# Experts' weighted sums: from a VectorE multiply-add to a ScalarE scaling and an accumulating DMA from GpSimd's queue

## The chip, the cores and the metric

The kernel runs on one core of a Trainium2 chip. The metric is the device time of one execution in microseconds (us). Three executions of the kernel before took 652.2, 653.46 and 654.13 us, so the median is 653.46 us.

## The reference, cut to what matters

Three stages follow one another. A windowed attention (2 batches, 8 heads, 576 positions) gives `x` of 1152 tokens by 512. A mixture of four experts, all of them used for every token, turns `x` into a weighted sum. A last stage with a rational activation turns that into the output.

```
p = domain_probs / (domain_probs.sum(-1, keepdims=True) + 1e-09)
out = np.zeros((N, D), dtype=np.float32)          # N = 1152, D = 512
for e in range(E):                                # E = 4, F = 1024
    h = np.maximum(x @ w1[e], 0.0)
    out += p[:, e:e + 1] * (h @ w2[e])            # the weighted sums of the change
x = out
h = x @ w_in                                      # 512 -> 2048
g = (a0 + a1 h + a2 h^2 + a3 h^3) / (1 + |b0||h| + |b1| h^2 + 1e-06)
return g @ w_out                                  # 2048 -> 512
```

## The kernel before, in words

The 1152 tokens are nine tiles of 128 (t = 0 to 8) in three chunks of three (c = 0 to 2). Each matrix operand is split into a high and a low part, and three products are summed for each, so that float32r matmuls give nearly float32 precision. The hidden units are walked in groups g of 512: groups 0 to 7 belong to the four experts (two groups each), groups 8 to 11 to the last stage. A group has two halves u = 2g and 2g + 1.

For each group and chunk the kernel does three things. `h_bank` (line 321) makes the first products of a half in PSUM tiles called `ps_h`, 24 matmuls for a half and chunk. `h_relu` has ScalarE write the rounded positive part `hh` (line 334), and VectorE the rest `hl` (line 335). `o_tile` (through `o_half`, line 358) makes the second product of one token tile, 12 matmuls into one PSUM bank `ps_o`; the pool `pso` has two such banks. Then `o_sum` adds that bank into the token tile's accumulator `acc[t]`, an SBUF tile of 128 by 512 float32. For the experts, group 0 is written by a VectorE multiply (line 380), and groups 1 to 7 are added by one VectorE instruction that multiplies the bank by the token's expert weight and adds it to `acc[t]` (line 382). That is 7 groups by 9 tiles, 63 instructions.

Between the experts and the last stage stands the turn: `x2_turn` (line 403) has TensorE transpose the three finished accumulators of a chunk into PSUM, and `x2_split` cuts the result into the high and low operands of the next products. The order there, written out by hand at `g == NG1` and just before it, is: the transposes of chunk 0 (tiles 0 to 2); `o_tile` of tiles 3, 4, 5 and then 6 of group 7; the transposes of chunk 1 (tiles 3 to 5); the first products of two halves of chunk 0; `o_tile` of tiles 7 and 8; the first products of one half of chunk 1; and the first transposes of chunk 2 (tiles 6 to 8).

The instruction order of every engine is the order in which the code issues it (`tc.manual_schedule()`); each engine runs its own queue in order and waits on semaphores for the others. SP's queue issues the weight loads (line 88 loads the last stage's weights, 1024 KB each) and the stores. Through groups 0 to 7 a side job (`convert`, lines 119 to 172) turns the last stage's 64-bit weights into float32 on VectorE and ScalarE, two steps after each `o_tile` and `h_step`. GpSimd works in the attention alone (line 260); its queue is empty afterwards.

Of the kernel before, what the change touches and what calls it, by code (L numbers as in the profile page):

```python
# [18 lines left out]
F32 = mybir.dt.float32  # L19
# [3 lines left out]
AF = mybir.ActivationFunctionType  # L23
ALU = mybir.AluOpType
# [5 lines left out]
NT, DM = 1152, 512  # L30
# [14 lines left out]
def body(ctx, tc, qkv, mask, dp, w1, w2, w1d, w2d, coef, out):  # L45
    nc = tc.nc
# [3 lines left out]
    hp = ctx.enter_context(tc.tile_pool(name="hp", bufs=6))  # L50
    wp = ctx.enter_context(tc.tile_pool(name="wp", bufs=4))
    dram = ctx.enter_context(tc.tile_pool(name="dram", bufs=1, space=DRAM))
    rawp = ctx.enter_context(tc.tile_pool(name="rawp", bufs=4))
    pso = ctx.enter_context(tc.tile_pool(name="pso", bufs=2, space=PSUM))
    psh = ctx.enter_context(tc.tile_pool(name="psh", bufs=2, space=PSUM))
# [2 lines left out]
    def h_tile(count=[0]):  # L58

        count[0] += 1  # L60
        pool = third[0] if third and count[0] % 3 == 0 else psh
        return pool.tile([128, 2, 512], F32, tag="h", name="ps_h")
# [250 lines left out]
    acc = {}  # L313
# [26 lines left out]
    def rows(t):  # L340
        if t < 3:
            return [(0, 128, S // 3 + 128 * t)]
        if t == 3:
            return [(0, 128, 0)]
        if t == 4:
            return [(0, 64, 128), (64, 64, S)]
        return [(0, 128, 128 * t)]
# [14 lines left out]
    def o_bank():  # L362
        return pso.tile([128, 512], F32, tag="o", name="ps_o")

    def o_tile(g, t, ps=None):

        held, ps = ps is not None, ps if ps is not None else o_bank()
        for v in range(2):
            o_half(g, t, v, ps)
        if not held:  # L370
            o_sum(g, t, ps)

    def o_sum(g, t, ps):
        first = g in (0, NG1)
        if first:
            acc[t] = accp.tile([128, DM], F32, tag=f"acc{t}", name=f"acc{t}")
        if g < NG1:
            pe = p_sb[:, t, g // 2:g // 2 + 1]
            if first:
                nc.vector.tensor_scalar(out=acc[t], in0=ps, scalar1=pe, scalar2=None, op0=ALU.mult)  # L380
            else:
                nc.vector.scalar_tensor_tensor(  # L382
                    out=acc[t], in0=ps, scalar=pe, in1=acc[t], op0=ALU.mult, op1=ALU.add
                )
        elif first:
            nc.vector.tensor_copy(acc[t], ps)
        else:
            nc.vector.tensor_tensor(out=acc[t], in0=ps, in1=acc[t], op=ALU.add)  # L388
        if g == NG - 1:
            for a, n, r in rows(t):  # L390
                nc.sync.dma_start(out[r:r + n, :], acc[t][a:a + n, :])
# [79 lines left out]
    with tc.manual_schedule():  # L471
# [326 lines left out]
        ps = h_tile()  # L798
        ps = [ps[:, 0], ps[:, 1], o_bank()]
# [8 lines left out]
        for t in range(3):  # L808
            o_sum(g, 3 + t, ps[t])
        ps = [h_tile()[:, 0], h_tile()[:, 0], o_bank()]  # L810
        for v in range(2):
            for t in range(3):
                o_half(g, 6 + t, v, ps[t])
                if v == 1:
                    o_sum(g, 6 + t, ps[t])
# [109 lines left out]
```

## Time and profile before

| | |
|---|---|
| median of three executions | 653.46 us (652.2 to 654.13) |
| span of the profiled execution, first to last instruction | 650.9 us |
| TensorE (PE) busy | 639.6 us, 98% |
| VectorE (DVE) busy | 485.0 us, 75% |
| ScalarE (ACT) busy | 277.7 us, 43% |
| GpSimd (POOL) busy | 17.0 us, 3% |
| granted TensorE clock | 1.000 |

For the profiled execution the profile gives the span alone and no time of its own besides; the span lies 2.6 us below the median of the three timed executions, and that difference holds what lies around the span. In the profile, PE is TensorE's matmuls and PEld its weight loads, which overlap them. A row of the timeline begins with the start and the duration in us; a bracket at its end gives the idle time before it and what ended that.

### The profile page before, as it was taken

How to read it: one execution, taken by the hardware profiler on the slowest of the kernel's cores; microseconds unless marked ns; L12 is line 12 of the kernel's file. 1: busy time of each engine (PE TensorE's matmuls, PEld its weight loads, DVE VectorE, ACT ScalarE, POOL GpSimd, SP SyncE). 2: the span in 40 equal slices, each digit the busy share in tenths (PEclk: the TensorE clock that was granted, in tenths of full speed). 3: DMA queues.
4: the chain of work that ended last, by engine and by line, in shares of the span. 5: the costliest groups of instructions: out<-in, count | busy, mean ns of one | idle time of the engine just before them, and what ended most of it. 6: DMA issues, size and time to landing. Idle time of an engine off the chain costs nothing.

```text
span 650.9 us, 9488 instructions
## 1 busy us (share of the span) xinstructions
PE 639.6 (98%) x3838; PEld 574.6 (88%) x3839; DVE 485.0 (75%) x693; ACT 277.7 (43%) x518; POOL 17.0 (3%) x30
## 2 busy tenths in 40 slices
PE   8989999999999999999999999999999999999996
PEld 4878898999999999999999999989999999999985
DVE  6767326867867777777767766436999999999986
ACT  5887412413313323223233232115666555556651
POOL 2311100000000000000000000000000000000000
PEclk9999999999999999999999999999999999999999
DMA  9973011545344444454553572431230330300012
GB/s 293 275 219 104 21 65 47 195 148 172 120 161 149 142 163 137 154 162 115 176 162 102 161 254 93 167 130 38 92 130 1 129 130 2 129 1 1 0 49 97
DMA packets 25707, 79.53 MB, mean 122 GB/s; under 512 B 2720, under 2 KB 3232, under 8 KB 23616
## 3 DMA queue, kind: packets, MB, share of 16 engines
q1 hardware_dynamic: 25376, 78.77, 37.4%
q8 instruction: 30, 0.49, 0.3%
q10 hardware_dynamic: 288, 0.16, 0.1%
q14 instruction: 13, 0.11, 0.0%
HBM read 59.79 MB, written 19.14 MB: 121 GB/s over the span
## 4 chain that ended last, share of the span: by engine, by line
PE 94%; DVE 3%; ACT 2%; issue 0%; DVEq 0%; ACTq 0%
PE ps_h L321 46%; PE ps_o L358 43%; PE ps_v L285 1%; ACT pr L250 1%; PE ps_s L271 1%; PE ps_s L218 1%; PE ps_h L403 1%; PE ps_h L547 1%; PE ps_h L358 0%; DVE u L447 0%; DVE acc L388 0%; DVE u L460 0%; DVE sq L455 0%; DVE sq L452 0%; DVE sq L437 0%
## 5 line engine op out<-in xcount | busy, mean ns | idle before, releaser
L321 PE MATMUL ps_h<-xh,w 128*128 128x384 f32 x1152 | 301.7, 336 | 2.0 <-DVE hl L335 2.0
L358 PE MATMUL ps_o<-w,hh 128*128 128x512 f32 x832 | 224.3, 391 | 0.0
L321 PEld LDWEIGHTS ps_h<-xh,w 128*128 128x128 f32 x1152 | 208.8, 188 | 3.9 <-DVE hl L335 2.2
L321 PE MATMUL ps_h<-xl,w 128*128 128x384 f32 x576 | 192.7, 335 | 0.0
L358 PEld LDWEIGHTS ps_o<-w,hh 128*128 128x128 f32 x832 | 155.1, 188 | 31.1 <-ACT hh L334 0.4
L358 PE MATMUL ps_o<-w,hl 128*128 128x512 f32 x416 | 128.6, 390 | 0.0
L321 PEld LDWEIGHTS ps_h<-xl,w 128*128 128x128 f32 x576 | 108.1, 188 | 1.2
L335 DVE SCALAR_TENSOR_TENSOR hl<-ps_h,hh 128x768 fp32r<-128x768 f32 x48 | 45.9, 957 | 73.2 <-ACT hh L334 73.2
L358 PEld LDWEIGHTS ps_o<-w,hl 128*128 128x128 f32 x416 | 78.0, 188 | 16.9 <-DVE hl L335 0.4
L334 ACT ACTIVATE hh<-ps_h 128x768 fp32r<-128x768 f32 x48 | 39.1, 814 | 120.6 <-PE ps_h L321 120.5
L168 ACT CAST w<-f 128x512 fp32r<-128x512 f32 x32 | 19.9, 621 | 123.6 <-DVE f L165 123.6
L382 DVE SCALAR_TENSOR_TENSOR acc<-ps_o,p_sb,acc 128x512 f32<-128x512 f32 x63 | 47.1, 748 | 11.4 <-PE ps_o L358 11.4
L106 DVE TENSOR_TENSOR w<-raw,w 128x512 fp32r<-128x512 f32 x64 | 42.0, 695 | 0.7 <-ACT w L105 0.6
L170 DVE TENSOR_TENSOR w<-f,w 128x512 fp32r<-128x512 f32 x32 | 22.2, 692 | 22.8 <-ACT w L168 22.8
L441 ACT ACTIVATE ab<-sq,cbias 128x768 f32<-128x768 f32 x24 | 22.6, 944 | 37.2 <-DVE sq L437 37.0
L105 ACT CAST w<-raw 128x512 fp32r<-128x512 f32 x60 | 34.0, 617 | 0.0
L432 ACT ACTIVATE sq<-ps_h 128x768 f32<-128x768 f32 x24 | 19.3, 803 | 32.4 <-PE ps_h L321 32.4
L250 ACT ACTIVATE pr<-pr,mx 128x80 f32<-128x80 f32 (+1 forms) x84 | 29.7, 356 | 6.5 <-DVE mx L243 6.3
L437 DVE SCALAR_TENSOR_TENSOR sq<-sq,absb,ab 128x768 f32<-128x768 f32 x24 | 24.3, 1011 | 3.8 <-ACT ab L433 3.8
L467 DVE TENSOR_TENSOR hl<-u,hh 128x768 fp32r<-128x768 f32 x24 | 22.9, 954 | 5.4 <-ACT hh L464 5.4
L447 DVE SCALAR_TENSOR_TENSOR u<-u,na,ps_h 128x768 f32<-128x768 f32 x24 | 24.3, 1014 | 0.9
L460 DVE SCALAR_TENSOR_TENSOR u<-u,na,sq 128x768 f32<-128x768 f32 x24 | 24.3, 1013 | 0.4
(64 smaller groups left out, 521.0 us busy)
## 6 DMA issues: line engine op xcount, KB each, us to landing
w<-w SPq DMA_DIRECT2D x32, 512.0 KB, 3.6
w<-w SPq DMA_DIRECT2D x16, 1024.0 KB, 5.4
raw<-in_w_dram SPq DMA_DIRECT2D x30, 512.0 KB, 5.9
x<-in_w1d_dram SPq DMA_DIRECT2D x16, 512.0 KB, 5.1
x<-in_w2d_dram SPq DMA_DIRECT2D x16, 512.0 KB, 5.2
out_dram<-acc SPq DMA_DIRECT2D x8, 256.0 KB, 2.2
v<-in_qkv_dram SPq DMA_DIRECT2D x6, 320.0 KB, 6.7
qk<-in_qkv_dram SPq DMA_DIRECT2D x4, 448.0 KB, 5.3
```

Of the source, the lines that this page charges most:

```text
L105: (nc.vector.tensor_copy if early else nc.scalar.copy)(w[:, 0, s], raw[:, s])
L106: nc.vector.tensor_tensor(out=w[:, 1, s], in0=raw[:, s], in1=w[:, 0, s].bitcast(F32), op=ALU.subtract)
L250: nc.scalar.activation(pr[:, j, i], pr[:, j, i], AF.Exp, scale=-1.0, bias=self.mx[:, j, i:i + 1], accum_out=self.total[:, j, i:i + 1],)
L321: nc.tensor.matmul(ps[:, i, :TC], lhsT=a[:, k, f], rhs=b[:, k], start=k + n == 0, stop=k + n == 5,)
L334: nc.scalar.activation(hh, ps[:, :, :TC], AF.Relu)
L335: nc.vector.scalar_tensor_tensor(out=hl, in0=ps[:, :, :TC], scalar=0.0, in1=hh.bitcast(F32), op0=ALU.max, op1=ALU.subtract,)
L358: nc.tensor.matmul(ps, lhsT=a[:, i, tk], rhs=b[:, i], start=v + n == 0, stop=v + n == 6)
L382: nc.vector.scalar_tensor_tensor(out=acc[t], in0=ps, scalar=pe, in1=acc[t], op0=ALU.mult, op1=ALU.add)
L437: nc.vector.scalar_tensor_tensor(out=self.sq, in0=self.sq, scalar=absb[:, 1:2], in1=self.ab, op0=ALU.mult, op1=ALU.add,)
L447: nc.vector.scalar_tensor_tensor(out=self.u1, in0=self.u1, scalar=na[:, 1:2], in1=ps, op0=ALU.add, op1=ALU.mult)
L460: nc.vector.scalar_tensor_tensor(out=self.u1, in0=self.u1, scalar=na[:, 0:1], in1=self.sq, op0=ALU.add, op1=ALU.mult)
L467: nc.vector.tensor_tensor(out=self.hl, in0=self.u1, in1=self.hh.bitcast(F32), op=ALU.subtract)
```

## The change

In groups 1 to 7 the one VectorE instruction goes. In its place ScalarE multiplies the bank by the token's expert weight and writes the product into an SBUF tile `add`, one of four in a new pool. GpSimd's queue then issues a DMA that adds `add` to `acc[t]` in SBUF. Group 0 and the last stage stay as they were.

```
+    tmpp = ctx.enter_context(tc.tile_pool(name="tmpp", bufs=4))
...
             if first:
                 nc.vector.tensor_scalar(out=acc[t], in0=ps, scalar1=pe, scalar2=None, op0=ALU.mult)
             else:
-                nc.vector.scalar_tensor_tensor(
-                    out=acc[t], in0=ps, scalar=pe, in1=acc[t], op0=ALU.mult, op1=ALU.add
-                )
+                add = tmpp.tile([128, DM], F32, tag="add", name="add")
+                nc.scalar.activation(add, ps, AF.Copy, scale=pe)
+                nc.gpsimd.dma_start(acc[t], add, accum_op=ALU.add)
```

One line is added ahead of `o_sum`, so that line 403 of the kernel before is line 404 after, and so on. The rows below are instructions in the order of one engine's queue, with what each waits for: DMASW is a DMA of GpSimd's queue, PE, DVE and Activation the engines. On ScalarE before, at the turn (`hh` are group 7's last relus, `xh0` and `xh1` the splits of chunks 0 and 1, `sq` and `ab` the last stage's first activations):

```order
L334 ACTIVATE hh_3984<-ps_h_3959 128x768 [waits PE_49]
L334 ACTIVATE hh_4015<-ps_h_3990 128x768 [waits PE_49]
L411 CAST xh0_4019<-ps_h_4021 128x768 [waits PE_49]
L411 CAST xh0_4019<-ps_h_4030 128x768 [waits PE_49]
L411 CAST xh1_4099<-ps_h_4101 128x768 [waits PE_49]
L411 CAST xh1_4099<-ps_h_4110 128x768 [waits PE_49]
L432 ACTIVATE sq_4144<-ps_h_4119 128x768 [waits DMAHW0_49,DMAHW3_49,DVE_49,PE_49]
```

On ScalarE after, at the same place:

```order
L335 ACTIVATE hh_4101<-ps_h_4076 128x768 [waits PE_49]
L335 ACTIVATE hh_4132<-ps_h_4107 128x768 [waits PE_49]
L412 CAST xh0_4136<-ps_h_4138 128x768 [waits PE_49]
L412 CAST xh0_4136<-ps_h_4147 128x768 [waits PE_49]
L384 ACTIVATE add_4169<-ps_o_4156,p_sb_87 128x512 [waits DMASW5_49,PE_49,Activation_49]
L384 ACTIVATE add_4185<-ps_o_4172,p_sb_87 128x512 [waits DMASW6_49,PE_49,Activation_49]
L384 ACTIVATE add_4201<-ps_o_4188,p_sb_87 128x512 [waits DMASW7_49,PE_49,Activation_49]
L384 ACTIVATE add_4221<-ps_o_4208,p_sb_87 128x512 [waits DMASW0_49,PE_49,Activation_49]
L412 CAST xh1_4224<-ps_h_4226 128x768 [waits PE_49]
L412 CAST xh1_4224<-ps_h_4235 128x768 [waits PE_49]
```

The four scalings of tiles 3 to 6 have come between the splits of chunks 0 and 1; their DMASW wait is for the DMA that read the same `add` tile four uses ago. On VectorE the four rows of line 382 that stood there are gone. On TensorE before, the transposes of chunk 1 (`acc3` to `acc5`) behind the last matmuls of tile 6:

```order
L358 MATMUL ps_o_4085<-w2_3609,hl_4016 128x512 x2
L403 MATMUL ps_h_4101<-ident_81,acc3_1153 128x128 [waits PE_49]
L403 MATMUL ps_h_4101<-ident_81,acc4_1178 128x128
L403 MATMUL ps_h_4101<-ident_81,acc5_1212 128x128 [waits DVE_49]
L403 MATMUL ps_h_4101<-ident_81,acc3_1153 128x128
L403 MATMUL ps_h_4101<-ident_81,acc4_1178 128x128
L403 MATMUL ps_h_4101<-ident_81,acc5_1212 128x128
```

On TensorE after:

```order
L359 MATMUL ps_o_4208<-w2_3708,hl_4133 128x512
L404 MATMUL ps_h_4226<-ident_84,acc3_1156 128x128 [waits DMASW1_49,PE_49]
L404 MATMUL ps_h_4226<-ident_84,acc4_1181 128x128 [waits DMASW2_49]
L404 MATMUL ps_h_4226<-ident_84,acc5_1215 128x128 [waits DMASW3_49]
L404 MATMUL ps_h_4226<-ident_84,acc3_1156 128x128
L404 MATMUL ps_h_4226<-ident_84,acc4_1181 128x128
L404 MATMUL ps_h_4226<-ident_84,acc5_1215 128x128
```

TensorE's own order is the same. The third transpose waited for VectorE's addition to tile 5 and now waits for the DMA that adds to it; the transposes of chunks 0 and 2 changed in the same way. The matmul that opens a `ps_o` bank again after such a sum waits for ScalarE where it waited for VectorE. On GpSimd's queue the 63 DMAs stand behind the attention's last instruction of line 260 (261 after), with nothing between them.

## Rows read from the trace of the kernel before

**Rows 1.** The page: busy time by engine, and the span in 40 slices.

```profile
PE 639.6 (98%) x3838; PEld 574.6 (88%) x3839; DVE 485.0 (75%) x693; ACT 277.7 (43%) x518; POOL 17.0 (3%) x30
...
PE   8989999999999999999999999999999999999996
```

**Rows 2.** The chain that ended last: start us, us, what; groups 6 and 7.

```profile
385.05 8.34 PE ps_h L321 x48
393.40 8.20 PE ps_o L358 x36
401.60 8.34 PE ps_h L321 x48
409.94 8.20 PE ps_o L358 x36
```

**Rows 3.** Stages: us, then busy us and instructions of each engine, clock, DMA.

```profile
115.00:455.00 340.00, 340.00 (x1736) 310.12 (x1735) 241.72 (x372) 101.70 (x158) 0.00 (x0) 1.00 0.45 147
```

**Rows 4.** Groups by line, 115 to 455 us: busy us, mean ns | idle before.

```profile
L382 DVE SCALAR_TENSOR_TENSOR acc<-ps_o,p_sb,acc 128x512 f32<-128x512 f32 x63 | 47.1, 748 | 11.4 <-PE ps_o L358 11.4
...
L334 ACT ACTIVATE hh<-ps_h 128x768 fp32r<-128x768 f32 x38 | 31.0, 815 | 104.8 <-PE ps_h L321 104.7
...
L168 ACT CAST w<-f 128x512 fp32r<-128x512 f32 x31 | 19.3, 621 | 119.6 <-DVE f L165 119.6
```

**Rows 5.** Line 382: min/median/max ns, first and last start us.

```profile
L382 DVE SCALAR_TENSOR_TENSOR acc<-ps_o,p_sb,acc x63: 742/750/753, 114.9 to 454.6; 128x512 f32<-128x512 f32 x63
```

**Rows 6.** Timeline of TensorE at 37.7 us.

```profile
37.74 0.44 PE L321 MATMUL ps_h<-xh,w 128*128 128x384 f32 x1 [1.96 <-DVE hl L335]
```

**Rows 7.** Timeline of VectorE at the turn.

```profile
418.19 0.75 DVE L382 SCALAR_TENSOR_TENSOR acc<-ps_o,p_sb,acc 128x512 f32<-128x512 f32 x1 [1.27 <-PE ps_o L358]
...
436.04 0.75 DVE L382 SCALAR_TENSOR_TENSOR acc<-ps_o,p_sb,acc 128x512 f32<-128x512 f32 x1 [1.97 <-PE ps_o L358]
```

**Rows 8.** Timeline of TensorE at the turn: transposes, and tile 8's last matmuls.

```profile
426.33 1.47 PE L403 MATMUL ps_h<-ident,acc 128*128 128x128 f32 x12
...
435.61 0.39 PE L358 MATMUL ps_o<-w,hl 128*128 128x512 f32 x1
...
438.56 1.48 PE L403 MATMUL ps_h<-ident,acc 128*128 128x128 f32 x12
...
453.26 0.62 PE L358 MATMUL ps_o<-w,hl 128*128 128x512 f32 x2
...
457.90 0.82 PE L403 MATMUL ps_h<-ident,acc 128*128 128x128 f32 x6
```

**Rows 9.** Timeline of ScalarE at the turn, and a run of four casts.

```profile
118.60 2.17 ACT L105 CAST w<-raw 128x512 fp32r<-128x512 f32 x4
...
439.42 1.50 ACT L411 CAST xh<-ps_h 128x768 fp32r<-128x768 f32 x2 [10.68 <-PE ps_h L403]
...
452.90 0.83 ACT L464 CAST hh<-u 128x768 fp32r<-128x768 f32 x1 [1.76 <-DVE u L460]
```

**Rows 10.** The page's DMA issues: count, KB each, median us to landing.

```profile
w<-w SPq DMA_DIRECT2D x32, 512.0 KB, 3.6
w<-w SPq DMA_DIRECT2D x16, 1024.0 KB, 5.4
...
out_dram<-acc SPq DMA_DIRECT2D x8, 256.0 KB, 2.2
```

**Rows 11.** Line 391's stores, and the slowest transfer of the DMA view.

```profile
DMA to landing us min/median/max: 2.0/2.4/2.9
...
dp_sb<-in_dp_dram SPq DMA_DIRECT2D x1, 18.0 KB, 10.0
```

**Rows 12.** GpSimd's instructions by line: busy us, mean ns | idle before.

```profile
L260 POOL TENSOR_TENSOR pr<-pr,rs 128x288 f32<-128x288 f32 (+1 forms) x24 | 16.3, 702 | 55.1 <-DVE rs L258 55.1
```

**Rows 13.** SP's issues at the turn, and two stages (last columns: DMA share, GB/s).

```profile
452.55 1.68 SPq L88 DMA_DIRECT2D w<-w  x2
...
435.00:440.00 5.00, 5.00 (x30) 4.32 (x29) 1.50 (x2) 0.58 (x1) 0.00 (x0) 1.00 0.00 0
...
455.00:458.00 3.00, 3.00 (x19) 2.96 (x18) 2.96 (x4) 1.56 (x2) 0.00 (x0) 1.00 0.98 371
```

## The prediction, made before the changed kernel ran

> **What bounds the kernel now.** I read the page's busy times first, then the chain that ended last, then the stretch that the change touches, and last the timeline at the turn from the experts to the last stage. TensorE is busy for 639.6 of 650.9 us, in every slice of the page from start to end [rows 1]. The chain is TensorE's own queue: a first product of 48 matmuls (8.34 us), then three `o_tile` of 12 (8.20 us, 2.73 us each), and again [rows 2]. All 63 instructions that the change replaces start between 114.9 and 454.6 us [rows 5]. In that stretch TensorE is busy for 340.00 of 340.00 us at a granted clock of 1.00, which is the upper level of 2.4 GHz; VectorE is busy for 241.72, ScalarE for 101.70, GpSimd for nothing [rows 3]. So a bank `ps_o` or an `hl` is never late for TensorE there. The one long wait for VectorE's `hl`, 1.96 us, is at 37.74 us, before the first replaced instruction [rows 6].
>
> **The change part by part.**
>
> *Removed:* 63 multiply-adds of 748 ns, 47.1 us of VectorE [rows 4]. They lie beside TensorE, which waits for none of them, so this returns 0 us; VectorE falls from 241.7 to about 195 us of the 340.
>
> *Added on ScalarE:* 63 scalings of 128x512 from PSUM. No row shows one. A cast of the same width takes 621 ns, a relu from PSUM of one and a half times the width 815 ns [rows 4]. I take 0.62 us: 39 us in all, and ScalarE goes from 102 to 141 us of 340. What hides it is that TensorE needs a bank again only when the next tile's 12 matmuls are over, 2.73 us later. Behind a scaling on ScalarE stand relus, casts of weights and the side job's steps. These wait no longer for the bank than VectorE's own instructions did. The worst that I find ahead of a scaling is the run of four casts of 2.17 us [rows 9]: 2.17 + 0.62 = 2.79 us, at most 0.06 us over the cover, at one place. I count 0.
>
> *Added on GpSimd and the DMA engines:* 63 transfers of 256 KB. Each is issued by a queue that is otherwise empty. An `add` tile is used again four tiles later, an accumulator nine tiles later, and between two groups of three tiles lies a first product of 8.34 us [rows 2]. So any transfer that lands within some 10 us is late for nobody in groups 1 to 6.
>
> *Moved onto the path:* at the turn TensorE reads the accumulators themselves. What was a VectorE instruction with a wait that ended in time is now scaling, issue, transfer and landing. Let L be the time from the end of a scaling to when TensorE may read the accumulator.
>
> - Tiles 3 to 5. VectorE starts on tile 5 at 436.04, just behind the bank's last matmul (435.61 + 0.39) [rows 7, 8]. ScalarE is idle there for 10.68 us [rows 9], so it starts at the same time and ends at 436.66. The transposes start at 438.56, twelve in 1.48 us with 0.27 us for the last [rows 8], so one each 0.11 us, and tile 5 is the third: needed at 438.78. The cover is 2.12 us and the wait L - 2.12. The DMA engines are idle from 435 to 440 [rows 13].
> - Tiles 6 to 8. Tile 8's last matmul ends at 453.26 + 0.62 = 453.88 [rows 8]. ScalarE's `hh` cast, which stood from 452.90 to 453.73 [rows 9], can only come earlier without VectorE's addition ahead of it, so the scaling runs from 453.92 to 454.54. It is needed as the third transpose behind 457.90, at 458.12 [rows 8]. The cover is 3.58 us. But SP issues two weight loads of 1024 KB at 452.55, and the DMA engines are 98% busy from 455 to 458 [rows 13]. This transfer has to share them. An estimate: between nothing and the 3.2 us by which a 1024 KB load (5.4) exceeds a 256 KB store (2.2) [rows 10]; I take the middle, about 1.5 us. The wait is L + 1.5 - 3.58 = L - 2.08. The loads hang on TensorE's progress, so a first wait moves both alike.
> - Tiles 0 to 2. VectorE starts on tile 2 at 418.19, so the scaling ends at 418.81; needed at 426.33 + 0.22 = 426.55 [rows 7, 8]. The cover is 7.7 us, and the wait is 0 unless L is longer than that.
>
> *The size of L.* No row has a transfer of GpSimd's queue or one that adds. The lower bound is the fastest 256 KB store of SP's queue, 2.0 us; the upper bound is the slowest transfer of the trace, 10.0 us [rows 11]. An adding transfer has to read 256 KB of `add` and 256 KB of `acc`; the 512 KB transfers to and from the scratch land in 3.6 us [rows 10]. For the issue by GpSimd I add 0.4 us, between nothing and one of its instructions of 702 ns [rows 12]. I take L = 4.0 us.
>
> By the Trainium skill, page "DMA: Bandwidth & Descriptors", section "Anatomy of one DMA — SWDGE (gpsimd) path", a transfer issued by GpSimd takes about 2.0 us and its bytes over 436 GB/s. An estimate from that page is 2.6 us for 256 KB, with waits of 0.5 and 0.5 us and a time of 654.5 us; no run here shows a transfer of that queue.
>
> *The sum.* (4.0 - 2.12) + (4.0 - 2.08) = 1.88 + 1.92 = 3.8 us. Behind the turn TensorE is just as full as before it, so nothing gives this back. Against the profiled execution: 650.9 + 3.8 = 654.7 us of span, and with the 2.56 us by which the median lies above the span, 653.46 + 3.8 = 657.3 us. In general the sum is twice L less 4.2 us.
>
> **The rivals.** What a measurement of this kernel can tell from no change is about 0.3%, 2.0 us; that is L = 3.1 us.
>
> 1. *The transfer is hidden by the cover that is there.* If an addition in SBUF lands like SP's 256 KB stores, in 2.2 us [rows 10], and GpSimd's issue adds less than a microsecond, L stays at or below 3.1 us: waits of 0 to 2.0 us in all and a time of 653.5 to 655.4 us, not slower by the bound above. For it: the destination is SBUF, and the engines are idle at the first place [rows 13]. Against it: the transfer reads two operands, and the second place is crowded. The point from which it decides is tile 5's transpose, about 2 us behind its scaling.
> 2. *The queue is much slower,* L from 5.5 to 10 us, as transfers of this trace under traffic are [rows 11]. Then the waits are 6.8 to 15.8 us, and from 7.7 us on tiles 0 to 2 wait too (2.3 us at 10): 660 to 672 us. Against it: little traffic at the first place.
> 3. *Banks come free too late.* If ScalarE, which has relus and casts ahead of the scalings, missed the 2.73 us by 0.5 us in each of the 21 groups of three tiles, TensorE would wait 10.5 us: 664 us. Against it: ScalarE has 238 of 340 us free [rows 3], and its waits for VectorE (119.6 us at line 168 [rows 4]) get shorter when VectorE has less to do.
> 4. *Faster.* It would need a TensorE wait in the stretch that a freer VectorE removes; the rows show none [rows 3]. Only scatter is left.
>
> **How the numbers follow.** The forecast (L between 3.1 and 5.5 us, 655.4 to 660.3 us) has 0.45, rival 1 0.35, rival 2 0.12, rival 3 0.04, rival 4 0.04. Slower is 0.45 + 0.12 + 0.04 = 0.61, within 0.3% 0.35, faster 0.04. The time is that of the forecast, 657.3 us. The range reaches down to 652.8, no wait at all and half a microsecond of scatter, and up to 662.7 us, which is L = 6.7 us; above it lie most of rival 2 and rival 3, below it rival 4 and some scatter. The forecast's own range is 655.4 to 660.3 us.
>
> **What would show it.** In the profile after: TensorE's waits at the transposes of chunks 1 and 2 with a DMA of `add` as releaser, about 1.9 us each and none at chunk 0; the view of DMA issues with 63 transfers of 256 KB landing 3.5 to 4.5 us behind their issue; between 115 and 425 us the chain of TensorE with the same 8.34 and 8.20 us; VectorE some 47 us less busy, ScalarE some 39 us more. I am wrong if the transposes start without a wait (rival 1), if the wait at chunk 0 appears too (rival 2), or if single pieces of 8.20 us have become longer (rival 3).

## The result and the profile after

The changed kernel takes 662.76 us, median of 4 runs (661.92 to 663.64), against 653.80 us for the kernel before (4 runs, 652.20 to 654.51): a ratio of 1.0145 with a 95% interval of 1.0128 to 1.0162 (the two medians alone give 1.0137). It is slower by 9.0 us, where I had forecast 3.8. The profiled execution has a span of 660.7 us against 650.9, so the trace has to account for 9.8 us.

The page of the changed kernel, parts 1, 2, 3 and 6:

```profile
span 660.7 us, 9665 instructions
...
PE 643.2 (97%) x3839; PEld 577.2 (87%) x3839; DVE 445.0 (67%) x630; ACT 318.4 (48%) x581; POOL 71.8 (11%) x93
...
PEclk9999999999999999999999999999799999999999
...
q1 hardware_dynamic: 25376, 78.77, 37.2%
...
q0 software_dynamic: 9072, 16.52, 14.4%
...
acc<-add POOLq DMA_DIRECT2D x63, 256.0 KB, 5.3
```

Against [rows 1], VectorE is less busy, ScalarE and GpSimd more, and a queue q0 is there. One slice of 40 has a lower TensorE clock: the 29th, 463 to 479 us. First the stretch of the experts, in stages (us; then busy us and instructions of PE, PEld, DVE, ACT, POOL; clock; DMA share; GB/s), and behind it the stages at the end of the turn:

```profile
115.00:425.00 310.00, 310.00 (x1577) 283.08 (x1576) 190.71 (x297) 128.19 (x203) 49.54 (x57) 1.00 0.76 203
...
460.00:465.00 5.00, 0.62 (x3) 0.18 (x1) 4.33 (x5) 4.88 (x6) 0.00 (x0) 0.86 0.98 290
465.00:470.00 5.00, 4.59 (x16) 4.59 (x17) 1.15 (x2) 0.00 (x0) 0.00 (x0) 0.50 0.01 3
470.00:475.00 5.00, 5.00 (x26) 4.53 (x25) 0.00 (x0) 2.44 (x4) 0.00 (x0) 0.96 0.00 0
```

TensorE is busy for 310.00 of 310.00 us while 57 of the 63 transfers are issued, so groups 1 to 6 lose nothing, as in [rows 3]. Then comes a stretch of 5 us in which it works for 0.62 us, and one in which it works at a granted clock of 0.50, the lower of its two levels (1.2 GHz). Its timeline at the three places where it reads the accumulators (start us, us, instruction; in brackets the idle time before and what ended it), which answers to [rows 8]:

```profile
426.55 1.47 PE L404 MATMUL ps_h<-ident,acc 128*128 128x128 f32 x12
...
438.78 0.38 PE L404 MATMUL ps_h<-ident,acc 128*128 128x128 f32 x2
440.72 1.31 PE L404 MATMUL ps_h<-ident,acc 128*128 128x128 f32 x10 [1.55 <-DMA acc<-add]
...
459.88 0.27 PE L404 MATMUL ps_h<-ident,acc 128*128 128x128 f32 x1
463.70 0.48 PE L404 MATMUL ps_h<-ident,acc 128*128 128x128 f32 x1 [3.56 <-DMA acc<-add]
465.41 1.11 PE L404 MATMUL ps_h<-ident,acc 128*128 128x128 f32 x4 [1.23 <-DMA acc<-add]
466.18 0.67 PE L322 MATMUL ps_h<-xh,w 128*128 128x384 f32 x1
...
472.36 1.09 PE L359 MATMUL ps_o<-w,hh 128*128 128x512 f32 x4
```

Chunk 0 (426.55) starts without a wait. Chunk 1 stops at its third transpose, the first that needs tile 5. Chunk 2 stops twice, before the second transpose (tile 7) and before the third (tile 8). The row `472.36` is the first second-product matmul behind chunk 2's transposes; between them lie 24 first-product matmuls, the first of them at 466.18. In the trace of before the same two points are:

```profile
458.47 0.42 PE L321 MATMUL ps_h<-xh,w 128*128 128x384 f32 x1
...
462.74 1.08 PE L358 MATMUL ps_o<-w,hh 128*128 128x512 f32 x4
```

So the account is, all in start times of TensorE's rows, after less before:

- Chunk 0 starts at 426.55 instead of 426.33: 0.22 us of drift over the stages before.
- Chunk 2 starts at 459.88 instead of 457.90 [rows 8], 1.98 later. Less the 0.22 that is 1.76 us from the first wait: 1.55 idle and about 0.2 beside it.
- From chunk 2's first transpose to row `472.36` it is 12.48 us; before, 457.90 to 462.74, it was 4.84. That is 7.64 us more: 3.56 + 1.23 = 4.79 idle, and 2.85 in which TensorE was not idle but took longer. Of the 2.85, 1.91 lie on the 24 matmuls alone (466.18 to 472.36 is 6.18 us; before, 458.47 to 462.74, 4.27). The other 0.94 lies on the transposes, and not all of it can be the clock: the first wait too cost 0.2 us beside its idle time, at a clock of 1.00.
- Together 0.22 + 1.76 + 7.64 = 9.62 of the 9.8 us; the other 0.2 us I leave open.

Why tile 7 and tile 8 came so late stands in four views. ScalarE's scalings of tiles 5, 7 and 8:

```profile
436.31 0.69 ACT L384 ACTIVATE add<-ps_o,p_sb 128x512 f32<-128x512 f32 x1 [2.03 <-PE ps_o L359]
...
453.17 0.69 ACT L384 ACTIVATE add<-ps_o,p_sb 128x512 f32<-128x512 f32 x1
...
455.89 0.69 ACT L384 ACTIVATE add<-ps_o,p_sb 128x512 f32<-128x512 f32 x1 [1.17 <-PE ps_o L359]
```

GpSimd's issues of the same three tiles:

```profile
437.40 0.86 POOL L385 DMA_DIRECT2D acc<-add  x1 [1.86 <-ACT add L384]
...
454.26 0.87 POOL L385 DMA_DIRECT2D acc<-add  x1 [13.27 <-ACT add L384]
...
456.98 0.86 POOL L385 DMA_DIRECT2D acc<-add  x1 [1.85 <-ACT add L384]
```

SP's issues of the two weight loads, 1024 KB each:

```profile
454.52 0.32 SPq L89 DMA_DIRECT2D w<-w  x1
...
455.88 0.32 SPq L89 DMA_DIRECT2D w<-w  x1
```

And the DMA view's queues (packets, MB, share of 16 engines' time), first from 455 to 459 us, where only one queue has packets:

```profile
q1 hardware_dynamic: 116, 0.95, 79.8%
```

then from 459 to 465.5 us:

```profile
q1 hardware_dynamic: 172, 1.15, 44.6%
q0 software_dynamic: 288, 0.52, 44.1%
```

Tile 5's transfer is alone: its scaling ends at 437.00, GpSimd issues at 437.40, it lands 3.3 us later, and TensorE goes on at 440.72. That is an L of 3.7 us. Tile 7's transfer was issued at 454.26, before either load, and landed at 463.70, 9.4 us later; tile 8's was issued at 456.98 and landed at 465.41, 8.4 us later. From 455 to 459 us SP's queue moved 0.95 MB and GpSimd's queue not one packet; its 0.52 MB (two tiles) came after 459.

### The profile page after: what moved, and what is told of

The parts are those of the page before. It is cut to its first block, busy times and chain, and to the rows that moved or that the text cites. A ratio compares the mean times of both kernels' runs of the same rounds, so it can differ in the third digit from the quotient of the medians.

```text
span 660.7 us, 9665 instructions
## 1 busy us (share of the span) xinstructions
PE 643.2 (97%) x3839; PEld 577.2 (87%) x3839; DVE 445.0 (67%) x630; ACT 318.4 (48%) x581; POOL 71.8 (11%) x93
## 4 chain that ended last, share of the span: by engine, by line
issue 43%; PE 42%; POOL 8%; DVE 3%; ACT 2%; DMA 1%; POOLq 0%; ACTq 0%
PE ps_h L322 20%; PE ps_o L359 17%; POOL acc L385 8%; PE ps_v L286 2%; DMA acc<-add 1%; PE ps_s L272 1%; PE ps_s L219 1%; ACT pr L251 1%; PE ps_h L548 1%; PE ps_h L359 0%; DVE w L107 0%; ACT pt L276 0%; DVE u L448 0%; DVE acc L389 0%; DVE u L461 0%
## 5 line engine op out<-in xcount | busy, mean ns | idle before, releaser
L385 POOL DMA_DIRECT2D acc<-add x63 | 54.7, 869 | 330.1 <-ACT add L384 309.4
L384 ACT ACTIVATE add<-ps_o,p_sb 128x512 f32<-128x512 f32 x63 | 43.4, 688 | 88.3 <-PE ps_o L359 62.2
```

What stands on the lines that cost most here:

```text
L384: nc.scalar.activation(add, ps, AF.Copy, scale=pe)
L385: nc.gpsimd.dma_start(acc[t], add, accum_op=ALU.add)
```

## The experiments

Each kernel was timed against the kernel before on the same chip; ratios have 95% intervals. Diffs are against the changed kernel. Group 7 is the last expert group, the one ahead of the turn.

**e2: group 7 as before.** VectorE keeps the nine multiply-adds of group 7; 54 transfers stay.

```
             elif g == NG1 - 1:
+                nc.vector.scalar_tensor_tensor(out=acc[t], in0=ps, scalar=pe, in1=acc[t], op0=ALU.mult, op1=ALU.add)
```

> Groups 1 to 6 as changed, group 7's nine sums by VectorE as before. Theory (all the loss is at the turn, 54 of the 63 transfers cost nothing): no wait at any transpose, 653.8 us, 653.0 to 654.6. Rival (the transfers also cost something in groups 1 to 6, by loads that come later or banks that come free later): above 655 us.

Measured: 653.48 us against 653.22, ratio 1.0004 (0.9994 to 1.0013). The 54 transfers land in a median of 5.5 us and cost nothing, and chunk 1's transposes are one run of twelve again:

```profile
438.73 1.47 PE L408 MATMUL ps_h<-ident,acc 128*128 128x128 f32 x12
```

**e3: only group 7 changed.** The reverse: `elif g < NG1 - 1:` keeps VectorE for groups 1 to 6; 9 transfers.

> Groups 1 to 6 by VectorE, only group 7 as changed. Theory (all the loss is at the turn): the same waits and half clock as with all 63, 662 to 663.5 us. Rival (part of it comes from the 54 earlier transfers): 655 to 660 us.

Measured: 662.23 against 653.22, ratio 1.0132 (1.0117 to 1.0147). TensorE waits 1.47, 3.50 and 1.11 us, and the clock from 465 to 470 us is 0.50. Nine transfers make the whole loss. With e2 this rules out the third rival, banks that come free too late, and any cost of the other 54 above the scatter (e2's interval is -0.4 to 0.8 us).

**e4: tiles 6 to 8 of group 7 as before.** `elif g == NG1 - 1 and t >= 6:` goes to VectorE, so that only the first wait can be there.

> As changed, but tiles 6 to 8 of group 7 by VectorE. Theory (two waits of different size, the half clock belongs to the second): first wait 1.5 us stays, second and half clock gone; 653.8 + 1.8 = 655.6 us, 655.0 to 656.3. Rival (the half clock comes from the first wait too or from the change in general): 657 us and more.

Measured: 655.43 against 653.22, ratio 1.0031 (1.0021 to 1.0042), 2.2 us. TensorE's row at chunk 1, and the stage behind it, clock 1.00:

```profile
442.77 1.31 PE L408 MATMUL ps_h<-ident,acc 128*128 128x128 f32 x10 [1.59 <-DMA acc<-add]
```

```profile
455.00:475.00 20.00, 20.00 (x107) 18.08 (x106) 17.28 (x20) 11.55 (x15) 0.00 (x0) 1.00 0.28 106
```

**e10: tiles 3 to 5 of group 7 as before.** `elif g == NG1 - 1 and 3 <= t < 6:` goes to VectorE; the second place alone.

> As changed, but tiles 3 to 5 of group 7 by VectorE. Theory (the waits add up, and the half clock belongs to the second alone): no first wait; second wait 4.8 us and a stretch at 0.50; 662.8 - 2.0 = 660.8 us, 660.0 to 661.8. Rival (it takes both waits together to bring the clock down): no stretch at 0.50, 658 to 659.5 us.

Measured: 661.37 against 653.12, ratio 1.0133 (1.0116 to 1.0150), 8.3 us. No wait at chunk 1; at chunk 2:

```profile
462.39 0.48 PE L408 MATMUL ps_h<-ident,acc 128*128 128x128 f32 x1 [3.15 <-DMA acc<-add]
...
464.60 1.12 PE L408 MATMUL ps_h<-ident,acc 128*128 128x128 f32 x4 [1.73 <-DMA acc<-add]
```

The second place needs no first wait ahead of it. Alone the two cost 2.2 and 8.3 us, together 9.0 (e3 and the changed kernel). The sum of 10.5 is 1.5 us more, about as much as the intervals leave open, so whether they simply add up is not shown.

**e1: the two loads later in SP's program.** Meant to take the loads away from tiles 7 and 8.

```
-                load_w2(u + 2)
+                if g != NG1: load_w2(u + 2)          # load_w2(u + 3) likewise
...
             o_step(g, 0, extra)
+            if g == NG1: load_w2(u + 2); load_w2(u + 3)
```

> Theory (the second wait, 4.8 us at the transposes of chunk 2, is contention with the two 1024 KB weight loads that SP issues at 454.5 and 455.9 us, and the half clock behind it follows from the wait): issued behind the turn, the loads leave the engines to the additions, which land 3.3 us after issue as at the first place; second wait 0.2 to 0.5 us, no stretch at granted clock 0.50; time 653.8 + 1.8 (first wait) + 0.3 = 655.9 us, 655.2 to 656.6. Rival (the adding transfer is slow there for a reason of its own, VectorE and ScalarE being busy at the time): second wait still over 4 us, time 662 to 663 us.

Measured: 663.31 against 653.22, ratio 1.0151 (1.0133 to 1.0169); waits 1.59, 3.50 and 2.40 us. The edit misfired. SP has nothing ahead of the loads to wait for, so they were issued as soon as their buffers were free. That is 0.25 us behind tile 7's transfer, as in the changed kernel (0.26); they start later only because the whole trace does (chunk 1's transposes start at 439.72 instead of 438.78):

```profile
455.23 0.87 POOL L385 DMA_DIRECT2D acc<-add  x1 [13.28 <-ACT add L384]
...
455.48 0.32 SPq L89 DMA_DIRECT2D w<-w  x1
```

It says nothing on the loads. A place later in the program is not a time later on a queue that does not wait.

**e9: the loads really later.** As e1, but the loads are issued from ScalarE's queue, behind ScalarE's own work of that step.

```
+            if g == NG1:
+                for v in (u + 2, u + 3):
+                    w2s[v] = wp.tile([128, 2, 1024], F32R, tag="w2", name="w2")
+                    nc.scalar.dma_start(w2s[v].bitcast(F32), scratch["w2", v])
```

> As changed, with the two 1024 KB loads at the turn issued from ScalarE's queue behind its work for the turn, so that they start some 15 us later; in e1 they had kept their time, 455.5 and 456.8 us, since SP's queue had nothing ahead of them to wait for. Theory (the second wait is the queueing behind these loads, and the half clock follows from that wait): the additions to tiles 7 and 8 land 3.3 us after issue, second wait 0 to 0.5 us, no stretch at 0.50; 653.5 + 1.8 + 0.3 = 655.6 us, 655.0 to 656.4. Rival (the adding transfers are slow there for another reason): second wait over 4 us, 662 to 663 us.

Measured: 656.00 against 653.12, ratio 1.0045 (1.0030 to 1.0059), 2.9 us instead of 9.0. The loads are issued at 475.36 and 475.73, and chunk 2's six transposes are one run with no wait:

```profile
441.34 1.31 PE L404 MATMUL ps_h<-ident,acc 128*128 128x128 f32 x10 [1.56 <-DMA acc<-add]
...
460.49 1.05 PE L404 MATMUL ps_h<-ident,acc 128*128 128x128 f32 x6
```

The stage that had a clock of 0.86 and TensorE busy for 0.62 us is full, and tiles 7 and 8 land 3.3 and 3.2 us behind their issue where it was 9.4 and 8.4. The median of the three transfers issued from 440 to 470 us (tile 6's among them) is 3.3 instead of 8.4:

```profile
460.00:465.00 5.00, 4.99 (x31) 4.72 (x30) 4.29 (x6) 4.28 (x6) 0.00 (x0) 1.00 0.10 17
```

```profile
acc<-add POOLq DMA_DIRECT2D x3, 256.0 KB, 3.3
```

This shows that the loads cause the second wait, and with it the half clock. The rival, that the second place is slow without the loads, falls.

**e11: e9 and e10 together.** Loads late, and tiles 3 to 5 on VectorE.

> e9 and e10 together: tiles 3 to 5 of group 7 by VectorE, the two loads from ScalarE's queue behind the turn, the other 60 transfers as changed. Theory (nothing else costs anything): wait at the transposes of chunk 2 at most 0.5 us, 653.5 + 0.3 = 653.8 us, 653.0 to 654.6. Rival (something of the loss is left elsewhere): 655.5 us or more.

Measured: 653.65 against 653.12, ratio 1.0005 (0.9996 to 1.0014). Tiles 6 to 8 still go by GpSimd's queue and are hidden:

```profile
457.73 1.12 PE L408 MATMUL ps_h<-ident,acc 128*128 128x128 f32 x6
```

The account is closed: taking away the first place's transfers and the second place's loads takes away all of the loss.

**e5: TensorE kept busy through the second wait.** 22 matmuls with no use ahead of chunk 2's transposes.

```
+                ps_f = o_bank()
+                for _ in range(22):
+                    nc.tensor.matmul(ps_f, lhsT=warm[:, :128], rhs=warm, start=True, stop=True)
                 x2_turn(2, 0)
```

> As changed, with 22 matmuls on a tile of zeros (results unused) ahead of the transposes of chunk 2, about 4.7 us of work in place of idle time. Theory (TensorE's clock falls because it idles; the half clock costs 1.9 us of matmuls and about 0.7 us of transposes): no stretch at 0.50, time 662.8 - 2.3 = 660.5 us, 660.0 to 661.3. Rival (the clock falls for another reason, or the wait alone is the price): still a stretch at 0.50, 662.5 us or more.

Measured: 661.49 against 653.73, ratio 1.0116 (1.0095 to 1.0137). TensorE's timeline, and the stage 465 to 470 us:

```profile
460.03 4.92 PE L754 MATMUL ps_o<-warm 128*128 128x512 bf16 x21
...
467.02 0.66 PE L404 MATMUL ps_h<-ident,acc 128*128 128x128 f32 x4 [1.85 <-DMA acc<-add]
467.43 0.42 PE L322 MATMUL ps_h<-xh,w 128*128 128x384 f32 x1
...
471.68 1.08 PE L359 MATMUL ps_o<-w,hh 128*128 128x512 f32 x4
```

```profile
465.00:470.00 5.00, 3.15 (x21) 2.98 (x20) 1.30 (x2) 0.14 (x1) 0.00 (x0) 1.00 0.02 6
```

The clock stays at 1.00, and the 24 first-product matmuls behind take 4.25 us (467.43 to 471.68) instead of 6.18. So the slow 24 matmuls come from the clock, and the clock from the idle time. In the total little of it is left: tile 8's transfer landed 9.8 us behind its issue here instead of 8.4, and 1.9 - 1.4 = 0.5 us is within the overlap of the two intervals.

**e6: a plain copy.** `nc.gpsimd.dma_start(acc[t], add)` without the addition. It leaves the earlier sums out: the accumulator holds the last expert's part only.

> All 63 transfers of GpSimd's queue write the tile add to the accumulator without adding; the earlier groups' sums are left out. Theory (an adding transfer is longer because it reads two operands): landing 2.3 to 2.8 us after issue at the first place instead of 3.3, first wait under 1.0 us, median landing of the 63 about 4.3 instead of 5.3. Rival (GpSimd's issue and the fixed part are all of it): 3.3 us and 5.3 us as before, same waits.

Measured: 659.62 against 653.73, ratio 1.0084 (1.0061 to 1.0107). Line 385 on GpSimd (duration ns min/median/max, first and last start; then landing us) in the changed kernel:

```profile
L385 POOL DMA_DIRECT2D acc<-add x63: 852/862/1010, 116.1 to 457.0; - x63
...
DMA to landing us min/median/max: 3.3/5.3/9.4
```

and with the plain copy:

```profile
L385 POOL DMA_DIRECT2D acc<-add x63: 536/536/767, 116.1 to 455.9; - x63
...
DMA to landing us min/median/max: 2.2/3.8/7.0
```

The addition makes the issue 0.33 us and the unhindered landing 1.1 us longer. The first wait falls to 0.56 us. Chunk 2's transposes now wait once, before the third (tile 8), and not for tile 7:

```profile
462.93 0.66 PE L404 MATMUL ps_h<-ident,acc 128*128 128x128 f32 x4 [3.73 <-DMA acc<-add]
```

Tile 8's copy lands 7.0 us behind its issue, so behind the loads a transfer of GpSimd's queue is late whether it adds or not. Tile 7's copy, issued at 453.21, again 0.26 us ahead of the first load, lands in 4.4 us instead of 9.4. Its 0.26 MB pass beside the first 0.54 MB of the loads, here from 454 to 457 us:

```profile
q1 hardware_dynamic: 66, 0.54, 65.4%
q0 software_dynamic: 66, 0.26, 21.5%
```

**e8: the turn's steps moved.** The loads as in e1, and chunk 1's and chunk 2's transposes each one first-product half later.

```
+            h_step(u, 0)            # was behind the transposes of chunk 1
...
+            if g == NG1: x2_turn(2, 0)    # was ahead of h_step(u + 1, 1)
```

> As changed, with the two weight loads behind the turn, the transposes of chunk 1 behind the next half's first products (4.2 us later) and those of chunk 2 behind one more half (4.2 us later). Theory (the cost is where TensorE reads the accumulators): cover 6 and 8 us for a latency of 3.7 us, no waits at the transposes, 653.8 us, 653.0 to 654.8. Rival (the later transposes make a new wait, the first products of chunk 1 for their operands or the last stage's chain on VectorE): 655 us or more.

Measured: 661.32 against 653.73, ratio 1.0108 (1.0090 to 1.0127). Chunk 1's wait is gone, but the next first product waits 3.40 us in its place:

```profile
447.61 0.41 PE L322 MATMUL ps_h<-xh,w 128*128 128x384 f32 x1 [3.40 <-issue]
```

The profile names no releaser for it. What ends just ahead of it, at 447.51, is VectorE's last read of the `ps_h` tile that the half put ahead of the transposes had filled:

```profile
446.50 1.01 DVE L448 SCALAR_TENSOR_TENSOR u<-u,na,ps_h 128x768 f32<-128x768 f32 x1
```

There are three such tiles, used in turn, and this first product is the fourth use, so it likely waits for that read. The granted clock from 450 to 455 us is 0.75. The loads again left 0.26 us behind tile 7's transfer (457.78), tile 8 landed 9.2 us behind its issue, and chunk 2's third transpose waited 1.79 us. More cover from order alone gave no clean repair.

**e7 and e12: the addition by GpSimd itself.** The scaling stays on ScalarE; instead of the transfer GpSimd adds in SBUF. e12 is the same kernel, timed again with 12 runs.

```
-                nc.gpsimd.dma_start(acc[t], add, accum_op=ALU.add)
+                nc.gpsimd.tensor_tensor(out=acc[t], in0=acc[t], in1=add, op=ALU.add)
```

> ScalarE scales as changed, GpSimd itself adds the tile to the accumulator in place of a DMA. An instruction of 128x512 there takes about 1.2 us by line 260's 702 ns for 288 to 320 columns. Theory (the loss is the transfer's latency and its sharing of the DMA engines): sum ready about 1.5 us behind the scaling, within the cover of 1.9 and 3.5 us; no waits, 653.8 us, 653.0 to 654.8. Rival (any chain over a third engine is late at the turn): a first wait of 1 us or more, above 655 us.

> e7 again with more rounds: GpSimd adds the tile itself. If its 0.16% is real, 652.5 to 653.0 us against 653.5 before, interval below 1; if it was scatter, the interval holds 1. No wait of TensorE was removed between the two in e7's trace, so scatter is what the theory says.

Measured: e7 652.83 against 653.73, ratio 0.9984 (0.9975 to 0.9994); e12 652.83 against 653.12, ratio 0.9999 (0.9990 to 1.0009). The 0.16% of e7 did not come again: it is the time of before, and no gain. Tile 5's addition, 1.28 us, is over before it is needed:

```profile
437.01 1.28 POOL L385 TENSOR_TENSOR acc<-acc,add 128x512 f32<-128x512 f32 x1 [1.44 <-ACT add L384]
```

The work of the change can move off VectorE at no cost; what costs is the transfer. No version that I ran beats the kernel before.

## Why the prediction was wrong

The sign and the place were right, the size was not: +9.0 us against +3.8, just above the range.

- *Groups 1 to 6, banks, accumulators: 0.* Right. TensorE's 310.00 of 310.00 us; e2 gives 0.3 us with an interval that holds zero. The chain's pieces keep their length; behind the turn the chain of after has:

```profile
514.51 8.34 PE ps_h L322 x48
522.86 8.20 PE ps_o L359 x36
```

- *VectorE's 47.1 us removed: worth nothing.* Right. Busy time falls by 40.0 us (485.0 to 445.0); by lines, where overlapping instructions count in full, by 46.6. ScalarE's scaling takes 0.69 us, not 0.62, and its busy time rises by 40.7 us.
- *L = 4.0 us.* Right: 3.7 us where nothing is in the way (0.4 to GpSimd's issue, 3.3 to landing). The row I took it from, 512 KB in 3.6 us, was the fit one. The estimate of 2.6 us by the Trainium skill, page "DMA: Bandwidth & Descriptors", section "Anatomy of one DMA — SWDGE (gpsimd) path", is near the plain copy's 2.3 us from issue to landing (e6), not near the 3.3 us of the transfer that adds.
- *First place: 1.88 us.* Right: 1.55 idle, 1.76 in all, and e4 alone 2.2.
- *Chunk 0: 0.* Right, no wait at 426.55.
- *Second place: 1.92 us.* This is the step that failed. The term was "between nothing and the 3.2 us by which a 1024 KB load (5.4) exceeds a 256 KB store (2.2)", taken at 1.5. It measured 5.1 us for tile 8 (8.4 instead of 3.3), outside both bounds, and 6.1 for tile 7 (9.4), which I had not priced at all. I had thought of a share of a busy resource, with half of the load in the way. What the runs show is a queue that gets nothing until the first load is nearly through: with the loads at 475 us (e9) the same transfers land in 3.3 us. By the Trainium skill, page "DMA: Bandwidth & Descriptors", section "Queues, rings and completion order", each DMA engine goes round the queues that have work for it, and drains a whole packet of some 9 to 17 descriptors from one before it turns to the next. The trace does not speak against that, since after 459 us both queues have packets. What the profile counts as packets are pieces of at most 8 KB, 288 for the two loads, so on average 9 for each load on each of the 16 DMA engines. Whether these 9 are one packet in the page's sense, so that an engine finishes its share of a load before it turns to the next queue, no run here shows.
- *The clock: not in the sum at all.* The 4.79 us of idle time brought the granted clock to 0.50, and the work behind it took 2.85 us more, of which 1.91 on the 24 matmuls are shown to be the clock's: e5, with as late a transfer but a busy TensorE, shows 1.00 and no slow matmuls. The first place's 1.55 us did not lower it (e4: 1.00).
- *"63 transfers landing 3.5 to 4.5 us behind their issue".* Wrong: 3.3 to 9.4, median 5.3. Within the groups that harms nobody.
- *The rivals.* From scaling to landing it was 3.7 us at the first place, which is the forecast, and 9.8 and 8.8 at the second (tiles 7 and 8), which is rival 2's 5.5 to 10 us. The prediction priced rival 2 for both places at once, and its argument against it looked at the first alone.

With the measured terms my own sum comes out: 1.76 at the first place; at the second 3.7 + 5.1 - 3.58 = 5.2, against 4.8 idle, and 2.85 for the slower work: 9.8 us. The terms are from the trace that they are to explain, so this shows only that no large one is missing.

Settled in part is why tile 7's transfer, issued before the loads, falls behind them. Without loads an adding transfer has its first packet 1.4 us behind its issue (e9: issued at 454.88, first packets from 456.3). Tile 7's would have begun at about 455.7, and the first load's packets began at 455.5. In e6 the order is reversed: the plain copy has packets from 454.3, the loads none before 454.45, and tile 7 is in time. The groups look the same: the transfer issued at 265.14 us, ahead of SP's next loads, lands in 3.3 us; the one at 267.91, 0.9 us behind SP's issue of a 512 KB load (267.04) and amid two more, in 7.5. So it seems that what counts is whose packets begin first, and not who issues first. That is an argument: e6 takes away the addition too, and no run changed the order alone. Whether GpSimd's queue is then started late or passed over, no run tells apart, and none splits the loads into smaller transfers.

## What to carry to other kernels

Before an addition on an idle engine is replaced by a transfer, find the consumer that reads the result soonest, and compare its cover with the landing time under the traffic that is there, not with that of a quiet moment: here TensorE waited for three of the 63 transfers, tiles 5, 7 and 8 of the last group, and lost 9 us. Price a collision with a large load as waiting for much of that load, not as sharing with it, and look at transfers issued shortly before it too. Where TensorE is otherwise never idle, add to a wait of several microseconds (here 3 and more; 1.6 left it at 1.00) what the lower clock costs behind it.

## What the runs showed of the hardware

- A 256 KB adding transfer within SBUF from GpSimd's queue holds GpSimd for 0.86 us and lands 3.3 us behind its issue; a plain one 0.54 and 2.3 us.
- Issued from 0.26 us ahead of the first of two 1024 KB loads of SP's queue to 2.5 us behind it, an adding one lands 8.4 to 9.8 us after issue (the changed kernel, e1, e5, e8, e10). The plain copy issued 0.26 us ahead lands in 4.4 us, the one 2.5 us behind in 7.0 (e6).
- TensorE idle for 1.55 us kept a clock of 1.00; idle for 3.56 and 1.23 us with one transpose between, it had 0.50 in the stage from 465 to 470 us and 0.96 in the next. Behind the single wait of 3.73 us of e6 the stage from 465 to 470 us has 0.73.
- GpSimd adds 128x512 in f32 in 1.28 us at the turn, so without a transfer the sum is ready 2.4 us sooner than by one (437.01 + 1.28 = 438.29 against 440.72).
